# Loading the keys of a multi-head attention in 1 MB transfers with 8192-byte rows, in a kernel that runs two attention blocks on one Trainium2 core

## The chip, the cores and the metric

The kernel runs on one core of one Trainium2 chip. Its time is device microseconds (us) of one execution. In the text, PE is the matrix engine, PEld its weight load, DVE the vector engine, ACT the scalar engine, POOL the GpSimd engine and SP the engine that issues the DMAs. A line number such as L976 is the line of the kernel before; where a line of the changed kernel is meant, the text says so.

## The reference

Two blocks with the same input shapes run side by side and their outputs are put next to each other. Both project x to 32 query heads, attend to a cache of 1024 keys, and project back. Block A shares each of 4 key/value heads among 8 query heads, block B has a key and value head for every query head, so its caches hold 134 MB each (16 x 32 x 1024 x 128 bf16).

```
# A: B, Sq, D = 16, 32, 1024; Hq, Hkv, Sk, Dh = 32, 4, 1024, 128
# B: the same, but with 32 key/value heads
q = (x @ wq).reshape(B, Sq, H, Dh).transpose(0, 2, 1, 3)
scores = einsum("bhqd,bhkd->bhqk", q, k_cache) * Dh ** -0.5
p = softmax(scores, axis=-1)
o = einsum("bhqk,bhkd->bhqd", p, v_cache)
out = o.transpose(0, 2, 1, 3).reshape(B, Sq, H * Dh) @ wo
# result: concatenate([out_A, out_B], axis=-1), bf16
```

## The kernel before

**How the order is made.** The kernel first records all operations in program order, each with its engine, its reads and writes, and the class of buffer it needs (`pr.add`). `list_schedule` then plans them: it takes assumed durations from the table `DUR`, assumed packet times from `PACKET`, and weights from `RANKS` and `TUNE`, and puts out one fixed order for each engine. Operations of engine "any" (copies out of PSUM, the scaling of the output) go to ACT or DVE as the plan sees fit. At run time each engine works through its list in order, and semaphores hold an operation until what it reads has come and what it overwrites has been read. So an instruction that waits holds up all that stands behind it on its engine. SP issues all input DMAs from one queue, in the planned order.

**Block A** works in 128 steps ("quads") of one batch and four heads: keys come in as 256 KB (L891), are transposed on PE (L969), scores are two matmuls of 512 columns (L995), then maximum (L1038), exponential with row sum (L1051), transposes of the probabilities (L1063), the product with the values (L1083), the scaling by 1/sum (L1174 or L1175), and a transpose back (L1182).

**Block B** works in 64 pairs of quads. A pair is two batches of four heads, 2 MB of keys and 2 MB of values. The steps of a pair are these.

- `st_dmaKB` (L910): four DMAs of 512 KB, two heads of one batch each. A partition holds 16 consecutive keys of one head, 4096 bytes, and two heads fill 128 partitions. `KB_sb` has 8 such tiles, so the next pair's keys are under way while one is worked on.
- `st_ktrB` (L976): DVE transposes each tile in place, in 32 x 32 blocks of four-byte elements (two bf16 values each).
- `st_scoresB` (L1027): 64 matmuls on 32 x 32 parts of the PE array, 512 columns each. A quad takes one head parity: its 128 rows are four (batch, head) combinations of 32 queries, its 1024 columns are all keys, in two PSUM banks.
- `st_max` and `st_exp`: one maximum over 1024 columns (L1038) and one exponential over 1024 columns with its row sum (L1051) for each quad.
- `st_ptB` (L1097): eight transposes of the pair's probabilities, and their copies to SBUF (L651, `PT_ev`).
- `st_pvB` (L1116): 64 matmuls of 64 x 64 by 256 columns. The values come in as four DMAs of 512 KB (L955) into `VB_sb`, which has 6 tiles.
- `st_recip` (L1165), `st_norm` (L1174, L1175): one reciprocal and one scaling of 256 columns for each quad.
- `st_otr` (L1190): two matmuls against a selecting matrix `rowsel` for each quad, and a copy into `OTB_sb`, from where `oproj` (L823) projects to the output.

The queries of B are projected by `qprojB` (L754), 128 tokens at a time with the tokens as rows, in `Qtok`. `qprepB_tr` (L765) then transposes them in blocks on DVE, and `qprepB_sh` (L778) moves the blocks between row groups by 16 matmuls with an identity, twice, and two copies into `QR`. This happens once for each group of two pairs, 32 times in all.

The last pair has a function of its own, `st_last` (L1135 and on), which finishes one half of its heads after the other. Near the end of the program tiles for keys and values are also put where weights and queries no longer are needed (`wq_sb`, `xT_sb`, `QT_sb`).

Of the kernel before, what the change touches and what calls it, by code (L numbers as in the profile page):

```python
# [19 lines left out]
NQT = 5  # L20
# [10 lines left out]
PE_MODE = {"scoresB": 2, "Qshuf": 2, "Qshuf2": 2, "PVB": 3, "PVBh": 3}  # L31
MODE_IN = 0.094
MODE_OUT = {0: 0.0, 2: 0.18, 3: 0.1}
PE_INSTR = {"scoresB": 32, "scoresA": 2, "PT_trA": 8, "PT_trB": 8, "PVA": 16, "PVB": 32, "PVBh": 32, "OT_tr": 2, "OT_trB": 4, "KTA_tr": 16, "Qshuf": 16, "Qshuf2": 16,
            "qprojA": 4, "qprojB": 4, "oprojA": 4, "oprojB": 4, "xT_tr": 16}
# [11 lines left out]
TUNE = (6, 7, 1, 5, 6, 8, 8, 8, 8, 8, 8, 11, 5, 15, 1, 9, 0, 1, 5, 1, 7, 14,  # L47
        15, 12, 12, 10, 12, 12, 15, 3, 12, 14, 7, 13, 13, 13, 13, 13, 7, 6, 10, 1, 12, 10,
        3, 12, 0, 11, 9, 12, 7, 13, 12, 11, 12, 3, 4, 10, 14, 9, 9, 10, 4, 0, 0)
# [3 lines left out]
QB0 = [0, 3, 6, 9]  # L53
QA0 = [13 + (i * 12) // 8 for i in range(8)]
QB1 = [27 + (i * 13) // 8 for i in range(8)]
QA_T = [10 + (i * 11) // 8 for i in range(8)]
QB_T = [23 + (i * 15) // 8 for i in range(8)]
# [3 lines left out]
    "scoresB": (0.232, 0.20), "scoresA": (0.216, 0.20), "PT_trA": (0.48, 0.22), "PT_trB": (0.48, 0.22), "PVA": (0.45, 0.22), "PVB": (0.437, 0.22), "PVBh": (0.22, 0.22),  # L61
    "OT_tr": (0.056, 0.22), "OT_trB": (0.112, 0.22), "KTA_tr": (0.45, 0.22), "Qshuf": (0.39, 0.20), "Qshuf2": (0.235, 0.20), "qprojA": (0.432, 0.20), "qprojB": (0.432, 0.20),
    "oprojA": (0.432, 0.20), "oprojB": (0.432, 0.20), "xT_tr": (0.45, 0.22),
    "exp": (1.10, 0.12), "PT_ev@act": (0.466, 0.13), "norm@act": (0.25, 0.13), "normB@act": (0.36, 0.13), "OT_ev@act": (0.11, 0.13), "OTB_ev@act": (0.17, 0.13), "KTA_ev@act": (0.466, 0.13),
    "qA_ev@act": (0.47, 0.13), "qB_ev@act": (0.478, 0.13), "QR_ev@act": (0.478, 0.13), "acc0@act": (0.47, 0.13), "acc0@dve": (0.58, 0.12), "xT_ev@act": (0.90, 0.13),
    "o_fin@act": (0.47, 0.13),
    "KBt_tr": (1.15, 0.11), "max": (1.12, 0.11), "recip": (0.06, 0.11), "norm@dve": (0.265, 0.13), "normB@dve": (0.40, 0.13), "PT_ev@dve": (0.58, 0.12),
    "OT_ev@dve": (0.13, 0.12), "OTB_ev@dve": (0.2, 0.12), "KTA_ev@dve": (0.58, 0.12), "QBt_tr": (0.345, 0.10), "acc+": (0.58, 0.12), "accF": (0.59, 0.12),
    "qA_ev@dve": (0.58, 0.12), "qB_ev@dve": (0.58, 0.12), "xT_ev@dve": (0.60, 0.12), "o_fin@dve": (0.58, 0.12), "QR_ev@dve": (0.58, 0.12),
# [3 lines left out]
PACKET = {"kb_dma": (4096, 0.1592), "vb_dma": (4096, 0.1592), "outh_dma": (1024, 0.049), "wqh_dma": (1024, 0.049)}  # L73
# [41 lines left out]
SLOTS = {"bank": 8, "P": 2, "P2": 1, "PT": 2, "PT2": 2, "stat": 8, "O": 2, "O2": 3}  # L115
# [12 lines left out]
class Prog:  # L128
# [63 lines left out]
    def _needs_wait(self, op, d):  # L192
        if d.dma_key is not None:
            return True
        if d.eng != op.eng:
            return True
        if (d.name, op.name) == ("Qshuf", "Qshuf2"):
            return True
        return op.eng in self.SELF_SYNC
# [49 lines left out]
    def list_schedule(self, lat=0.05, look=LOOK):  # L249
# [170 lines left out]
        while True:  # L420
# [61 lines left out]
            for u in users[best]:  # L482
                uo = ops[u]
                same_pe = (op.dma_key is None and beng == uo.eng and uo.eng == "pe" and uo.name != "Qshuf2")
# [68 lines left out]
def build(nc, pa, pb, out):  # L553
# [34 lines left out]
    with stack:  # L588
# [12 lines left out]
        Qtok = sb("Qtok", [P, NQT, CW], BF)  # L601
        QBt = sb("QBt", [P, CW], BF)
        QR = sb("QR", [P, 2, 4, 2, Dh], BF)
# [11 lines left out]
        P2_sb = sb("P2_sb", [P, SLOTS["P2"], 2 * Sk], BF)  # L615
        PT2_sb = sb("PT2_sb", [P, SLOTS["PT2"], Sk], BF)
        O2_sb = sb("O2_sb", [P, SLOTS["O2"], 2, Dh], BF)
        rowsel = sb("rowsel", [P, 2, P], BF)
        PT_sb = sb("PT_sb", [P, SLOTS["PT"], NCH, P], BF)
        O_sb = sb("O_sb", [P, SLOTS["O"], Dh], BF)  # L620

# [121 lines left out]

        def qprojB(m_, G):
            c2, mh = m_ // 2, m_ % 2
            lazy_flush(("wq", 1, c2))

            JS = 2 if DJ % 2 == 0 else 1
            v = Virt("bank", "pj")
# [653 lines left out]
```

## Time and profile before

| | |
|---|---|
| Time, median of 2 runs | 850.95 us (847.71 to 854.19) |
| Profiled execution, its own time | 851.34 us |
| Span in its profile | 849.5 us |
| Busy: PE, DVE, ACT, POOL | 783.0, 727.0, 623.6, 6.1 us |
| Mean granted PE clock | 0.995 |
| Moved by DMA | 341.68 MB, 402 GB/s over the span |

The span is what the profiler saw from the first instruction to the last; the execution's own time is 1.8 us longer. Busy time counts an instruction from its start to its end, so neighbours on one engine may overlap, and a busy PE need not be at its peak. A row of the groups names line, engine, operation, output and input, shape and count; behind the bar stand the busy time, the mean duration in ns, and the idle time just before them with what ended it.

### The profile page before, as it was taken

How to read it: one execution, taken by the hardware profiler on the slowest of the kernel's cores; microseconds unless marked ns; L12 is line 12 of the kernel's file. 1: busy time of each engine (PE TensorE's matmuls, PEld its weight loads, DVE VectorE, ACT ScalarE, POOL GpSimd, SP SyncE). 2: the span in 40 equal slices, each digit the busy share in tenths (PEclk: the TensorE clock that was granted, in tenths of full speed). 3: DMA queues.
4: the chain of work that ended last, by engine and by line, in shares of the span. 5: the costliest groups of instructions: out<-in, count | busy, mean ns of one | idle time of the engine just before them, and what ended most of it. 6: DMA issues, size and time to landing. Idle time of an engine off the chain costs nothing.

```text
span 849.5 us, 29749 instructions
## 1 busy us (share of the span) xinstructions
PE 783.0 (92%) x13056; PEld 522.6 (62%) x13056; DVE 727.0 (86%) x1018; ACT 623.6 (73%) x1363; POOL 6.1 (1%) x20
## 2 busy tenths in 40 slices
PE   7989999999898999998999988999899998899878
PEld 4456665666565566665666665666666666666655
DVE  1499987979799898987999898998999978998995
ACT  3497787778677777786788787677877867686874
POOL 1000000000000000000000000000000000000000
PEclk9999999999999999999999999999999999999999
DMA  9999999999999999999999999999999999999995
GB/s 339 415 412 414 411 411 410 405 393 394 416 384 412 409 395 415 416 398 412 414 392 408 411 392 416 415 416 405 410 402 415 412 414 415 415 400 414 416 418 226
DMA packets 112208, 341.68 MB, mean 402 GB/s; under 512 B 12048, under 2 KB 12304, under 8 KB 112080
## 3 DMA queue, kind: packets, MB, share of 16 engines
q1 hardware_dynamic: 111520, 337.95, 100.0%
q8 instruction: 103, 1.69, 0.7%
q0 software_dynamic: 560, 1.84, 0.5%
q14 instruction: 25, 0.20, 0.1%
HBM read 337.64 MB, written 2.10 MB: 400 GB/s over the span
## 4 chain that ended last, share of the span: by engine, by line
PE 55%; DVE 23%; ACT 14%; DMA 5%; issue 2%; SPq 1%; DVEq 0%; ACTq 0%
DVE stat L1038 10%; PE psum L1116 10%; PE psum L823 10%; DVE KB_sb L976 8%; ACT P_sb L1051 8%; PE psum L1027 6%; PE psum L1063 5%; PE psum L754 5%; PE psum L1097 5%; PE psum L1083 4%; DMA KB_sb<-in_B_k_cache_dram 4%; PE psum L995 4%; PE psum L735 4%; ACT PT_sb L651 2%; ACT O_sb L1174 1%
## 5 line engine op out<-in xcount | busy, mean ns | idle before, releaser
L1038 DVE TENSOR_REDUCE stat<-psum 128x1 f32<-128x1024 f32 x256 | 303.6, 1210 | 50.7 <-PE psum L995 31.5
L1051 ACT ACTIVATE P_sb<-psum,stat 128x1024 bf16<-128x1024 f32 x246 | 275.9, 1122 | 63.2 <-DVE stat L1038 59.7
L976 DVE STREAM_TRANSPOSE KB_sb<-KB_sb 128x1024 f32<-128x1024 f32 x240 | 286.6, 1222 | 6.2 <-DMA KB_sb<-in_B_k_cache_dram 6.0
L651 ACT COPY PT_sb<-psum 128x512 f32<-128x512 f32 x226 | 131.4, 604 | 35.2 <-PE psum L1063 22.0
L1116 PE MATMUL psum<-VB_sb,PT_sb 64*64 64x256 bf16 x3584 | 116.2, 271 | 8.6 <-ACT P_sb L1051 5.2
L1116 PEld LDWEIGHTS psum<-VB_sb,PT_sb 64*64 64x64 bf16 x3584 | 97.0, 107 | 27.7 <-issue 25.5
L1174 ACT ACTIVATE O_sb<-psum,stat 128x128 bf16<-128x128 f32 (+1 forms) x205 | 80.8, 417 | 43.2 <-PE psum L1083 23.1
L1063 PE MATMUL psum<-id,P_sb 128*128 128x128 f32 x512 | 88.7, 297 | 6.9 <-ACT P_sb L1051 4.1
L1063 PEld LDWEIGHTS psum<-id,P_sb 128*128 128x128 f32 x512 | 74.0, 208 | 25.2 <-ACT P_sb L1051 13.8
L995 PE MATMUL psum<-KTA_sb,QT_sb 128*128 128x512 bf16 x256 | 84.4, 384 | 3.1 <-ACT P_sb L1051 1.6
L1083 PE MATMUL psum<-VA_sb,PT_sb 128*128 128x128 bf16 x1024 | 78.8, 221 | 7.5 <-ACT P_sb L1051 2.6
L1083 PEld LDWEIGHTS psum<-VA_sb,PT_sb 128*128 128x128 bf16 x1024 | 63.2, 99 | 31.6 <-issue 12.0
L1027 PE MATMUL psum<-KB_sb,QR 32*32 32x512 bf16 x3840 | 73.3, 394 | 8.1 <-ACT P_sb L1051 4.6
L1097 PE MATMUL psum<-id,P_sb 128*128 128x128 f32 x472 | 76.2, 287 | 4.1 <-ACT P_sb L1051 3.5
L754 PE MATMUL psum<-wq_sb,xT_sb 128*128 128x512 bf16 x256 | 72.4, 394 | 3.3 <-DMA wq_sb<-in_B_wq_dram 1.6
L1097 PEld LDWEIGHTS psum<-id,P_sb 128*128 128x128 f32 x472 | 63.8, 193 | 17.3 <-ACT P_sb L1051 7.5
L823 PE MATMUL psum<-woB_sb,OTB_sb 128*128 128x512 bf16 x256 | 66.9, 380 | 2.4 <-ACT P_sb L1051 1.7
L1027 PEld LDWEIGHTS psum<-KB_sb,QR 32*32 32x32 bf16 x3840 | 43.8, 89 | 35.3 <-ACT P_sb L1051 8.3
L823 PE MATMUL psum<-woA_sb,OTA_sb 128*128 128x512 bf16 x256 | 62.8, 380 | 0.4 <-ACT OTA_sb L651 0.3
L735 PE MATMUL psum<-xT_sb,wq_sb 128*128 128x512 bf16 x192 | 54.2, 380 | 1.7 <-issue 1.2
L1051 ACT ACTIVATION_READ_ACCUMULATOR P_sb<-psum,stat 128x1 f32 x246 | 50.3, 205 | 0.0
L835 DVE TENSOR_TENSOR acc<-acc,psum 128x512 f32<-128x512 f32 x64 | 41.3, 675 | 9.6 <-PE psum L823 9.4
(74 smaller groups left out, 720.2 us busy)
## 6 DMA issues: line engine op xcount, KB each, us to landing
KB_sb<-in_B_k_cache_dram SPq DMA_DIRECT2D x240, 512.0 KB, 8.9
VB_sb<-in_B_v_cache_dram SPq DMA_DIRECT2D x234, 512.0 KB, 7.8
KA_sb<-in_A_k_cache_dram SPq DMA_DIRECT2D x64, 256.0 KB, 7.8
VA_sb<-in_A_v_cache_dram SPq DMA_DIRECT2D x64, 256.0 KB, 8.0
wq_sb<-in_B_wq_dram SPq DMA_DIRECT2D x16, 512.0 KB, 8.3
woB_sb<-in_B_wo_dram SPq DMA_DIRECT2D x32, 256.0 KB, 8.5
woA_sb<-in_A_wo_dram SPq DMA_DIRECT2D x32, 256.0 KB, 7.0
wq_sb<-in_B_k_cache_dram SPq DMA_DIRECT2D x16, 512.0 KB, 11.5
```

Source lines behind the costliest of these rows:

```text
L651: return e.copy(dst, src) if hasattr(e, "activation") else e.tensor_copy(dst, src)
L754: last = e.matmul(bank(v)[:, 0:CW], xT_sb[:, 1, j, G * P:(G + 1) * P], wq_sb[:, j, mh * CW:(mh + 1) * CW], start=(j == 0), stop=(j == DJ - 1))
L823: last = e.matmul(bank(v)[:, 0:OUTW], OT[:, gp, hh, :], wo_[:, hh, oh * OUTW:(oh + 1) * OUTW], start=(hh == 0), stop=(hh == nh - 1))
L976: pr.add("dve", lambda e: e.transpose(tile_k(x).bitcast(F32), tile_k(x).bitcast(F32)), writes=[home_k(x)], name="KBt_tr", rtag={home_k(x): ...
L995: pr.add("pe", lambda e, u=u: e.matmul(bank(vS[u]), qt[:, q.b, q.hh0:q.hh0 + 4, :].rearrange("p a q -> p (a q)"), KTA_sb[:, sl, u * 512:(u ...
L1027: last = e.matmul(bank(q.vS[g2])[32 * x:32 * x + 32, :].rearrange("p (s j) -> p s j", s=16), lhsT, rhs, start=(fp == 0), stop=(fp == 3), t ...
L1038: pr.add("dve", lambda e: e.tensor_reduce(stat[:, vst.idx, 0:1], both(vS), AXIS.XY, ALU.max, negate=True), writes=vS + [vst], name="max")
L1051: return e.activation(dst, src, ACTF.Exp, bias=stat[:, vst.idx, 0:1], scale=1.0, accum_out=stat[:, vst.idx, 1:2])
L1063: last = e.transpose(bank(vb)[:, m * P:(m + 1) * P], p32[:, m:Sk // 2:NPK], id32[:])
L1083: last = e.matmul(bank(vb)[:, 0:Dh], ptc_of(vPT, c, 0, P), VA_sb[:, kvs, c, :], start=(c == 0), stop=(c == NCH - 1))
L1097: last = e.transpose(bank(vb)[:, m * P:(m + 1) * P], p32[:, 4 * h + m:Sk:8], id32[:])
L1116: last = e.matmul(bank(q.vbo)[n0:n0 + 64, 0:2 * Dh].rearrange("p (i d) -> p i d", i=2), pt2_chunk(vPT, c, e0, n0), v2[e0:e0 + 64, :, c, :] ...
```

## The change

Keys of B now come in as one DMA for a batch and four heads: 1 MB, 128 rows of 8192 bytes. A head lies in 32 partitions (one row group of the PE array), and a partition holds 32 consecutive keys. The in-place transpose takes the four-byte elements in another order, so that the bf16 values of one block stand four apart instead of two. The rows of the scores change their meaning: a quad is now two heads of the pair's two batches, and the keys of a head are split into two halves (`u`) that lie in different rows, of which each has its own maximum for each of the two score banks.

What follows from that: the maximum over two banks gives two columns; the exponential is two instructions of 512 columns, each with its own bias and sum; the two halves of a head's keys are brought together by weights exp(m - m'), worked out on POOL with copies between groups of 32 partitions, one small exponential on ACT and one reciprocal on DVE (`st_weights`); the product with the values leaves twice as much output (the two key halves in separate rows, for two heads), so there are four scalings of 256 columns for each pair instead of two; and the selecting matmuls, now eight of 64 columns for each pair, also add the two halves.

The queries of B are projected with the weights as the stationary operand, every fourth column of them, so that the result already has the rows that the scores need (`QR`). The block transposes on DVE, the matmuls with the identity and their copies fall away. Values come in as before in 512 KB, but two tiles belong to one quad, and the products of a quad wait for its own two tiles alone. `st_last` goes, the last pair runs through the same functions quad by quad. The tables of the plan are set anew.

The core of the diff, without the tables of the plan:

```diff
-        def qprojB(m_, G):
+        def qprojB(m_, f, t0=0, tn=NTOK):
...
-                        last = e.matmul(bank(v)[:, 0:CW], xT_sb[:, 1, j, G * P:(G + 1) * P], wq_sb[:, j, mh * CW:(mh + 1) * CW], start=(j == 0), stop=(j == DJ - 1))
+                        last = e.matmul(bank(v)[:, 0:tn], wq_sb[:, j, mh * CW + f:(mh + 1) * CW:4], xT_sb[:, 1, j, t0:t0 + tn], start=(j == 0), stop=(j == DJ - 1))
...
+            evac(QR[:, m_ % 2, f, t0:t0 + tn], lambda: bank(v)[:, 0:tn], reads=[], writes=[v] + res, name="qB_ev" if tn > P else "qB0_ev",
-        def qprepB_tr(m_, G):
-        def qprepB_sh(m_, G):
...
+        def st_dmaKB(y):
+                src = pb["k"][q.b0 + y % 2, q.m * MS:(q.m + 1) * MS].rearrange("h (p s) d -> (h p) (s d)", s=32)
...
         def st_ktrB(x):
-            pr.add("dve", lambda e: e.transpose(tile_k(x).bitcast(F32), tile_k(x).bitcast(F32)),
+            pairs = lambda: tile_k(x).bitcast(F32).rearrange("p (s j g) -> p s g j", s=16, g=2)
+            pr.add("dve", lambda e: e.transpose(pairs(), pairs()),
...
# st_scoresB
-                            rhs = tile_k(4 * q.pn + x)[r0:r0 + 32, :].rearrange("p (s x) -> p s x", s=16)[:, :, o0:o0 + 63:2]
+                                rhs = kt_.rearrange("p (s v x) -> p s v x", s=16, v=2)[:, :, u, fp::4]
...
# st_max, block B
+                pr.add("dve", lambda e: e.tensor_reduce(stat2[:, q.vB.idx, 2 * q.e:2 * q.e + 2], both(vS), AXIS.X, ALU.max, negate=True),
# st_exp, block B
+            def emitB(e):
+                for g2 in range(2):
+                    k_ = 2 * q.e + g2
+                    src = bank(vS[g2]).rearrange("p (a s j) -> p j a s", a=2, s=8)
+                    dst = p2_of(vP)[:, g2 * 512:(g2 + 1) * 512].rearrange("p (j a s) -> p j a s", a=2, s=8)
+                    last = e.activation(dst, src, ACTF.Exp, bias=stat2[:, q.vB.idx, k_:k_ + 1], scale=1.0, accum_out=stat2[:, q.vB.idx, 4 + k_:5 + k_])
+                return last
+        def st_weights(qs, early):
+            vB = qs[0].vB
+            S = lambda a: stat2[:, vB.idx, 4 * a:4 * a + 4]
+            V = [q.vst for q in qs]
+            def swap(lo):
+                for b in range(4):
+                    pr.add("pool", lambda e, b=b: e.tensor_copy(stat2[32 * (b ^ 1):32 * (b ^ 1) + 32, vB.idx, lo + 8:lo + 12], stat2[32 * b:32 * b + 32, vB.idx, lo:lo + 4]),
+                           reads=V if lo else [q.vmx for q in qs], writes=[vB, "pool"], name="swap")
+            if early:
+                swap(0)
+                pr.add("pool", lambda e: e.tensor_tensor(S(4), S(0), S(2), ALU.subtract), writes=[vB, "pool"], name="small")
+                pr.add("pool", lambda e: e.tensor_scalar(S(4), S(4), 80.0, None, ALU.min), writes=[vB, "pool"], name="small")
+                pr.add("act", lambda e: e.activation(S(4), S(4), ACTF.Exp), writes=[vB], name="expw")
+                return
+            swap(4)
+            pr.add("pool", lambda e: e.tensor_tensor(S(4), S(4), S(3), ALU.mult), writes=[vB, "pool"], name="small")
+            pr.add("pool", lambda e: e.tensor_tensor(S(4), S(4), S(1), ALU.add), reads=V, writes=[vB, "pool"], name="small")
+            pr.add("dve", lambda e: e.reciprocal(S(5), S(4)), writes=[vB], name="recip")
...
# st_pvB, for one quad
-            for c0 in range(0, 16, 4):
+            for c0 in range(0, 8, 4):
+                            last = e.matmul(bank(vbo[h_])[n0:n0 + 64, i * 2 * Dh:(i + 1) * 2 * Dh], pt2_chunk(vPT, c, e0, n0),
+                                            v2[e0:e0 + 64, c * 2 * Dh:(c + 1) * 2 * Dh], start=(c == 0), stop=(c == 7), tile_position=(e0, n0))
+        def st_normB(q, vbo, h_, eng="any"):
+                    return e.activation(dst, src, ACTF.Copy, scale=stat2[:, vB.idx, 20 + k_:21 + k_])
+        def st_otrB(qs, vbo, h_, eng=None):
+                        last = e.matmul(bank(vbo[h_])[:, x * 64:x * 64 + 64], O2_sb[:, q.vO[h_].idx, u, :], rowsel[:, u, :], start=(u == 0), stop=(u == 1))
...
# pairB
+            for q in qs:
+                st_max(q)
+            st_weights(qs, True)
             for q in qs:
-                st_max(q)
                 st_exp(q)
-            st_ptB(qs)
+            st_weights(qs, False)
+            for q in qs:
+                st_ptB(q)
...
-            for q in qs:
-                st_recip(q)
-                st_norm(q)
-                st_otr(q)
+            for h_ in range(2):
+                for q in qs:
+                    st_normB(q, vbo, h_)
+                st_otrB(qs, vbo, h_)
```

## The prediction

> **What bounds the kernel now.** First the top of the page, to see which resource is full.
>
> ```profile
> span 849.5 us, 29749 instructions
> ...
> PE 783.0 (92%) x13056; PEld 522.6 (62%) x13056; DVE 727.0 (86%) x1018; ACT 623.6 (73%) x1363; POOL 6.1 (1%) x20
> ...
> DMA  9999999999999999999999999999999999999995
> GB/s 339 415 412 414 411 411 410 405 393 394 416 384 412 409 395 415 416 398 412 414 392 408 411 392 416 415 416 405 410 402 415 412 414 415 415 400 414 416 418 226
> ...
> q1 hardware_dynamic: 111520, 337.95, 100.0%
> ...
> PE 55%; DVE 23%; ACT 14%; DMA 5%; issue 2%; SPq 1%; DVEq 0%; ACTq 0%
> ```
>
> All 16 DMA engines are busy in every slice but the last. The trace's packet records say it more sharply: between 20 and 830 us the engines' time without a packet sums to only 2.3 us of all sixteen; after 830 us it is 8.5 us. So the transfers set the pace, at about 415 GB/s where packets are 4096 B, and the span is these bytes plus some 11 us of gaps, mostly the end.
>
> The chain of work in the last line names DMA for only 5%. The waits of the issuing queue explain that.
>
> ```profile
> SPq L955 <- PE psum L1116: 109.9, 36, 6.9
> SPq L891 <- PE psum L969: 80.9, 34, 6.7
> SPq L910 <- PE psum L1027: 57.0, 24, 5.1
> SPq L898 <- PE psum L1083: 54.2, 15, 8.3
> ```
>
> SP waits for PE to give a buffer back (us in total, times, longest), and the chain goes through PE there. Issues of 512 KB land after 7.8 to 8.9 us by the page, while the bytes need 1.25 us; the rest is mostly queue, which covers the waits. On the other side, by the landing events, a value tile's first matmul starts 14.5 us after its landing at the median, a key tile's transpose 2.4 us, and one in ten under 0.2 us. Keys are thus the link where transfers and compute touch. Compute has little room: PE is busy 47 of 50 us in the middle stretches. A gain in transfers is one only if PE, DVE and ACT keep up.
>
> **The change part by part.** The durations:
>
> ```profile
> L976 DVE STREAM_TRANSPOSE KB_sb<-KB_sb 128x1024 f32<-128x1024 f32 x240 | 286.6, 1222 | 6.2 <-DMA KB_sb<-in_B_k_cache_dram 6.0
> L1051 ACT ACTIVATE P_sb<-psum,stat 128x1024 bf16<-128x1024 f32 x246 | 275.9, 1122 | 63.2 <-DVE stat L1038 59.7
> ...
> L1051 ACT ACTIVATION_READ_ACCUMULATOR P_sb<-psum,stat 128x1 f32 x246 | 50.3, 205 | 0.0
> ...
> L1174 ACT ACTIVATE O_sb<-psum,stat 128x256 bf16<-128x256 f32 x82 | 36.5, 475 | 17.2 <-PE psum L1116 14.3 <-PE psum L995 1.4 <-DVE stat L1165 1.2
> ...
> L651 ACT CAST QR<-psum 128x512 bf16<-128x512 f32 x56 | 31.2, 599 | 7.3 <-PE psum L778 7.2
> ...
> L778 PE MATMUL psum<-QBt,ident 32*32 32x256 bf16 x512 | 20.1, 279 | 3.3 <-issue 0.4 <-ACT P_sb L1051 0.3
> ...
> L765 DVE STREAM_TRANSPOSE QBt<-Qtok 128x256 f32<-128x256 f32 x32 | 13.6, 425 | 13.6 <-ACT Qtok L649 13.6
> ...
> L640 POOL COPY rowsel<-ident 32x32 bf16<-32x32 bf16 x4 | 0.8, 202 | 0.2
> ```
>
> And the weight loads of L671, from the answer on that line (lowest/median/highest ns):
>
> ```profile
> L671 PEld LDWEIGHTS psum<-ident,acc x64: 142/147/171, 3.6 to 17.8; 128*128 128x128 bf16 x64
> ```
>
> *Key transfers, on the path.* Before, 256 DMAs of 128 packets of 4096 B, 2048 per DMA engine; after, 128 DMAs, 1024 packets of 8192 B per engine. Packet records give medians of 159 ns for 4096 B, 84 ns for 2048 B and, for the 25 packets of 8192 B that fetch instructions in mid-run, 309 ns. 2048 x 159 = 325.6 us becomes 1024 x 309 = 316.4: -9.2. Each DMA also ends in a 4-byte record of 9 ns per engine: 128 fewer, -1.2. Sum -10.4. The upper bound is 0: the DMA share in 50-us stretches reads 1.02 to 1.03, so packets overlap and a part of the fixed cost may already be hidden. I take -10, nearer the direct row, since all records of an engine sum to 853.9 us against 838 us not idle, a factor of only 0.98.
>
> *Later first key tile.* Both halves of 1 MB land together, so the first of two transposes may start 1.25 us later. The tiles' release does not change: one pair's scores read all four, before and after. A shift of the loop costs once, but one in ten starts is without slack: between 0 and 64 x 0.2 x 1.25 = 16 us. I take +2, about once more the present 2.3 us of gaps.
>
> *ACT, beside the path.* By the built order: 256 exponentials of 512 columns for 128 of 1024. A 512-column copy is 0.60 us, so each is 0.60 + 0.21, and 256 x 0.81 - 128 x 1.33 = +37. Scalings of 256 columns go from 82 to 211 on ACT: +61. The 64 small exponentials are not in the trace: at least a 64-column copy's 0.2, so +13, at most a 512-column copy's 0.6 (+38); 0.2 is nearer. Query copies on ACT fall from 84 to 28 (six of them short): -34. The plan moves other copies to DVE: -22. Sum +55: 679 us, 81% of 840.
>
> *DVE, beside the path.* -14 (L765), 64 fewer reciprocals -9, fewer query copies -3, moved copies about +25: 726 us, 86% of 840. Maxima keep 1024 elements and their 1.21 us. The key transposes read and write at 8-byte steps, which no row of DVE shows. The nearest is PE's weight load with 16-byte steps (L671): 147 ns at the median against 98 with contiguous data (L969), 50% more. Bounds: 0 and 256 x 0.61 = +156. I take 0, the step being half of L671's.
>
> The Trainium skill (Advanced Engine Details and Errata, SBUF Cachelines) states that two hits on each 16-byte line keep full speed, and fewer do not. Steps of 8 bytes give two, so by the rule these transposes cost 0 more; 16 bytes give one, and L671 agrees with that. No run here shows 8 bytes on DVE.
>
> *PE.* -20 (L778), with its switching of tile sizes. Selecting matmuls go from 252 to 512, half as wide: today 0.11 us of busy time each, so between 0 and +29. Projection issues 32 more short matmuls, +3. Between -17 and +12, and I take -5: 778 us, 93% of 840. Scores read at 8-byte steps, before at 4. Their 64 matmuls take 1.2 us a pair, so one of the 16 array parts has 0.3 us for a stream of 0.21 us (128 to 512 columns adds 0.16 us between L969 and L995): bounds 0 and, with doubled streams, +0.5 a pair, 32 us. I take 0. Weight loads of the projection at 8-byte steps (98 to 147 ns) hide behind 380-ns matmuls.
>
> *POOL, a new chain.* Twelve small operations a pair, each waiting for the one before: 202 ns (L640) to 311 ns (its slowest row), plus 0.1 to 0.2 between. The six after the second exponential end 2 us later, then the reciprocal on DVE; in that time PE transposes (0.7), a copy follows (0.6) and the products run (1.0), 2.3 us in all. So the chain hides behind these, barely; without the cover a scaling waits at the head of ACT's list, with the next maxima's exponentials behind it. The early chain ends in a small exponential on ACT in the same way.
>
> *SP* issues 128 fewer; *values* are freed per quad, earlier: both 0. The start stays full of transfers. From the last landing (840.8 us) to the end the order of work is much the same: 0, within 1 us.
>
> *Sum.* With less room on ACT I add +2 for further gaps: -10 + 2 + 2 = -6. The profiled execution took 851.3, so 845.3, and it lay 0.4 us above the median of the runs: 845 us.
>
> **The rivals.**
>
> *Compute takes the gain back.* For: the chain is 92% compute, and PE stays at 93%. If ACT's +55 shows by its 14% of the chain (+8) and PE's +12 by its 55% (+7), then -10 + 15 = +5: 856 us. Against: DVE waits for keys without slack, so a part does reach compute. The case that 8192-B data packets cost as much as two of 4096 belongs here: -1 + 4, 854 us.
>
> *Strided reading, slower.* The key transposes at 8-byte steps. It decides where DVE's 726 us pass 95% of 850, i.e. from +82 us, 0.32 us (26%) each. With the 50% of L671 DVE needs 882 us, and at 95% full the kernel takes 928. For: no row excludes it. Against: half the step of L671. Doubled score streams alone would give PE 810 us, some 870.
>
> *The POOL chain, slower.* If its operations take 0.5 us, the chain needs 4 us instead of 2, and the scalings of each pair hold ACT and two PSUM banks 0.5 to 2 us. ACT has 160 us free, so from about 1 us a pair it shows: at half of 64 x 0.75, 845 + 24 = 869 us. For: POOL is idle today, so its cost beside a busy DVE is unseen. Against: 202-ns rows.
>
> The Trainium skill (GPSIMD Engine Reference, Specifications) has POOL and DVE contend where DVE reads two SBUF inputs or runs in a two-port mode. DVE here reads one SBUF input at a time, so by it this chain stays short; no run here shows it yet.
>
> *A gain over 2%.* It would need 17 us, more than the transfers give; only a shorter end (8 us from the last landing) could add to it.
>
> **How the numbers follow.** Forecast 0.48 (its own range 839 to 851), gain taken back 0.26 (850 to 862), POOL 0.13 (855 to 885), strided reading 0.09 (865 to 930), over 2% 0.04. The range 837 to 870 leaves out most of strided reading, a third of POOL and a little at the bottom. Two per cent, 17 us, is about what a measurement of this kernel can tell from no change. Faster by more: 0.04. Slower by more (over 868): 0.08 of strided reading and 0.06 of POOL, 0.14. Within: 0.82.
>
> **What would show it.** Right: the GB/s row rises to 420 or more in slices full of keys, key packets at 309 ns, DMA still 9 in all slices; transposes at 1.22 us and scores at 0.39; POOL operations near 0.2 us; ACT near 680 us busy. Wrong: DMA digits below 9 in mid-run, SP or ACT waits that name POOL, L976's successor well above 1.22 us, or ACT's scalings with much idle time before them.

## The result and the profile after

The changed kernel takes 912.27 us (911.88 to 912.66, two runs) beside 850.95: a ratio of 1.072, 95% interval 1.068 to 1.076. It is 61 us slower; forecast were 845 us and a range of 837 to 870.

The top of the page of the changed kernel (the 40 slices are now 22.8 us each):

```profile
span 910.9 us, 30094 instructions
...
PE 840.0 (92%) x12768; PEld 531.5 (58%) x12768; DVE 734.3 (81%) x974; ACT 659.5 (72%) x1697; POOL 150.8 (17%) x788
...
DMA  9999999999999999899999999799999999999982
GB/s 341 419 416 411 389 377 339 386 415 356 359 383 419 372 371 401 327 396 389 368 361 410 380 405 400 271 384 396 397 346 418 412 389 408 396 375 403 384 338 99
...
q1 hardware_dynamic: 93088, 337.94, 95.2%
...
PE 63%; ACT 21%; DVE 9%; DMA 5%; issue 2%; SPq 1%; DVEq 0%; ACTq 0%
```

PE's busy time has grown by 57 us (783.0 to 840.0), the span by 61. The transfers no longer set the pace. The DMA row hardly shows it, with its digit still 9 in all but the last two slices and two in mid-run; the GB/s row does, with 271 to 390 in about half of its slices, where before all but the first and the last read 384 to 418. Queue q1 has gone from 100.0% to 95.2%. PE has gone from 55% of the chain to 63%, and ACT from 14% to 21%.

The groups with their shapes kept apart say which work grew. First the score matmuls of the kernel before, then the kernel after. There, L1009 are the score matmuls (L1027 before), L953 the key transposes, L1040 and L1033 the exponentials of B and A, L1142 the scalings of B, L1056 the POOL copies and L1067 the reciprocal behind them:

```profile
L1027 PE MATMUL psum<-KB_sb,QR 32*32 32x512 bf16 x3840 | 73.3, 394 | 8.1 <-ACT P_sb L1051 4.6 <-issue 0.9 <-ACT PT_sb L651 0.9
```

```profile
L953 DVE STREAM_TRANSPOSE KB_sb<-KB_sb 128x1024 f32<-128x1024 f32 x240 | 287.8, 1225 | 10.8 <-DMA KB_sb<-in_B_k_cache_dram 10.7
L1040 ACT ACTIVATE P_sb<-psum,stat 128x512 bf16<-128x512 f32 x236 | 160.0, 693 | 20.2 <-DVE stat L1024 19.3
L1009 PE MATMUL psum<-KB_sb,QR 32*32 32x512 bf16 x3840 | 124.2, 622 | 7.1 <-ACT P_sb L1033 3.7 <-issue 1.6 <-ACT OTB_sb L650 1.0
L1056 POOL COPY stat<-stat 32x4 f32<-32x4 f32 x512 | 92.0, 180 | 724.0 <-DVE stat L1024 525.8 <-ACT stat L1062 147.0 <-DVE stat L1163 27.9
L1142 ACT ACTIVATE O_sb<-psum,stat 128x256 bf16<-128x256 f32 x211 | 88.3, 480 | 18.2 <-PE psum L1128 15.4 <-DVE stat L1067 1.4 <-DVE stat L1163 0.8
L1067 DVE RECIPROCAL stat<-stat 128x4 f32<-128x4 f32 x64 | 10.3, 161 | 8.3 <-POOL stat L1066 8.1
```

The score matmuls are the row that stands out: 622 ns for 394, and 124.2 us busy for 73.3, with the same count and shape. The key transposes use the same 8-byte step and take 1225 ns for 1222. Two lines of each kernel's timeline (start in us, duration in us, a set of 64 score matmuls) show the same from outside, before first, then after:

```profile
197.40 1.22 PE L1027 MATMUL psum<-KB_sb,QR 32*32 32x512 bf16 x64
209.67 1.22 PE L1027 MATMUL psum<-KB_sb,QR 32*32 32x512 bf16 x64
```

```profile
197.34 2.02 PE L1009 MATMUL psum<-KB_sb,QR 32*32 32x512 bf16 x64
216.95 2.03 PE L1009 MATMUL psum<-KB_sb,QR 32*32 32x512 bf16 x64
```

A set is four rounds over the 16 array parts. In the trace nine in ten rounds start 222 to 251 ns apart before, 431 to 455 ns after. A set takes 0.82 us more at the median, and 64 sets give 52 us.

The waits, first one of before, then those of after: who waited for whom, the total in us, how often, the longest. DVE's maxima of B now wait 74.1 us for the scores, where they waited 16.0:

```profile
DVE stat L1038 <- PE psum L1027: 16.0, 25, 2.1
```

```profile
DVE stat L1024 <- PE psum L1009: 74.1, 58, 3.3
...
SPq L931 <- PE psum L1128: 204.6, 77, 7.3
...
SPq L883 <- PE psum L1009: 69.7, 28, 6.3
```

SP too waits longer for PE to give value tiles (L931, L1128 are the products) and key tiles (L883) back: 204.6 us for 109.9, and 69.7 for 57.0. Before, the GB/s row stayed up through such waits; now it dips.

### The profile page after: what moved, and what is told of

Read it like the earlier page. It is cut to its first block, busy times and chain, and to the rows that moved or that the text cites. A ratio compares the mean times of both kernels' runs of the same rounds, so it can differ in the third digit from the quotient of the medians.

```text
span 910.9 us, 30094 instructions
## 1 busy us (share of the span) xinstructions
PE 840.0 (92%) x12768; PEld 531.5 (58%) x12768; DVE 734.3 (81%) x974; ACT 659.5 (72%) x1697; POOL 150.8 (17%) x788
## 3 DMA queue, kind: packets, MB, share of 16 engines
q1 hardware_dynamic: 93088, 337.94, 95.2%
## 4 chain that ended last, share of the span: by engine, by line
PE 63%; ACT 21%; DVE 9%; DMA 5%; issue 2%; SPq 1%; DVEq 0%; ACTq 0%
PE psum L1009 14%; PE psum L1128 12%; ACT P_sb L1040 10%; PE psum L796 10%; PE psum L1111 6%; PE psum L1078 5%; DVE stat L1024 4%; PE psum L1098 4%; DMA KB_sb<-in_B_k_cache_dram 4%; PE psum L972 4%; PE psum L734 3%; PE psum L754 3%; ACT P_sb L1033 3%; DVE KB_sb L953 2%; ACT O_sb L1142 2%; PE psum L945 2%
## 5 line engine op out<-in xcount | busy, mean ns | idle before, releaser
L953 DVE STREAM_TRANSPOSE KB_sb<-KB_sb 128x1024 f32<-128x1024 f32 x240 | 287.8, 1225 | 10.8 <-DMA KB_sb<-in_B_k_cache_dram 10.7
L1056 POOL COPY stat<-stat 32x4 f32<-32x4 f32 x512 | 92.0, 180 | 724.0 <-DVE stat L1024 525.8
L1024 DVE TENSOR_REDUCE stat<-psum 128x2 f32<-128x1024 f32 x128 | 150.9, 1218 | 74.3 <-PE psum L1009 74.1
L1040 ACT ACTIVATE P_sb<-psum,stat 128x512 bf16<-128x512 f32 x236 | 160.0, 693 | 20.2 <-DVE stat L1024 19.3
L1021 DVE TENSOR_REDUCE stat<-psum 128x1 f32<-128x1024 f32 x128 | 154.2, 1208 | 12.9 <-PE psum L972 12.2
L1033 ACT ACTIVATE P_sb<-psum,stat 128x1024 bf16<-128x1024 f32 x128 | 144.4, 1128 | 23.8 <-DVE stat L1021 22.4
L1009 PE MATMUL psum<-KB_sb,QR 32*32 32x512 bf16 x3840 | 124.2, 622 | 7.1 <-ACT P_sb L1033 3.7
L1128 PE MATMUL psum<-VB_sb,PT_sb 64*64 64x256 bf16 x3584 | 116.8, 272 | 0.2
L1128 PEld LDWEIGHTS psum<-VB_sb,PT_sb 64*64 64x64 bf16 x3584 | 91.0, 107 | 23.8 <-issue 15.8
L1142 ACT ACTIVATE O_sb<-psum,stat 128x256 bf16<-128x256 f32 x211 | 88.3, 480 | 18.2 <-PE psum L1128 15.4
L1111 PE MATMUL psum<-id,P_sb 128*128 128x128 f32 x472 | 82.5, 299 | 13.9 <-ACT P_sb L1040 11.2
L1078 PE MATMUL psum<-id,P_sb 128*128 128x128 f32 x512 | 89.1, 298 | 4.4 <-ACT OTB_sb L650 1.4
L1078 PEld LDWEIGHTS psum<-id,P_sb 128*128 128x128 f32 x512 | 73.3, 208 | 26.9 <-issue 9.2
L1009 PEld LDWEIGHTS psum<-KB_sb,QR 32*32 32x32 bf16 x3840 | 48.4, 88 | 52.8 <-issue 23.2
L754 PE MATMUL psum<-xT_sb,wq_sb 128*128 128x512 bf16 (+2 forms) x288 | 71.6, 365 | 3.6 <-DMA wq_sb<-in_B_wq_dram 2.8
L1171 ACT ACTIVATE O_sb<-psum,stat 128x128 bf16<-128x128 f32 x111 | 42.1, 380 | 35.0 <-PE psum L1098 31.5
```

What stands on the lines that cost most here:

```text
L953: pr.add("dve", lambda e: e.transpose(pairs(), pairs()), writes=[home_k(x)], name="KBt_tr", rtag={home_k(x): x}, wtag={home_k(x): ("T", x)})
L1009: last = e.matmul(bank(q.vS[g2])[n0:n0 + 32, :].rearrange("p (s j) -> p s j", s=16), QR[r0:r0 + 32, gp, fp, tok:tok + 32], rhs, start=(fp ...
L1021: pr.add("dve", lambda e: e.tensor_reduce(stat[:, vst.idx, 0:1], both(vS), AXIS.XY, ALU.max, negate=True), writes=vS + [vst], name="max")
L1024: pr.add("dve", lambda e: e.tensor_reduce(stat2[:, q.vB.idx, 2 * q.e:2 * q.e + 2], both(vS), AXIS.X, ALU.max, negate=True), writes=vS + [q ...
L1033: return e.activation(dst, src, ACTF.Exp, bias=stat[:, vst.idx, 0:1], scale=1.0, accum_out=stat[:, vst.idx, 1:2])
L1040: last = e.activation(dst, src, ACTF.Exp, bias=stat2[:, q.vB.idx, k_:k_ + 1], scale=1.0, accum_out=stat2[:, q.vB.idx, 4 + k_:5 + k_])
```

## The experiments

Each kernel was timed against the kernel before on the same chip; ratios carry their 95% intervals, and differences in us are between medians. The kernel before lay between 849.54 and 851.78 us on these chips, so that much of a difference between two experiments can be the chip's.

| kernel | us | ratio |
|---|---|---|
| e1: changed, scores two values apart | 872.95 | 1.027 (1.022 to 1.031) |
| e2: before, four apart | 890.09 | 1.048 (1.044 to 1.051) |
| e3: e1, keys in 4096-byte packets | 873.34 | 1.028 (1.025 to 1.032) |
| e5: changed, plan knows the score time | 953.98 | 1.123 (1.117 to 1.129) |
| e6: e1, one exponential a quad | 862.24 | 1.015 (1.013 to 1.017) |
| e7: e1, no weights on POOL | 873.07 | 1.028 (1.024 to 1.032) |
| e8: e1, order searched anew | 877.29 | 1.030 (1.026 to 1.033) |
| e9: before, exponentials in halves | 874.73 | 1.028 (1.024 to 1.033) |
| e11: changed, plan knows, order searched anew | 891.42 | 1.046 (1.042 to 1.049) |
| e12: e6, scalings of 16 columns | 859.89 | 1.009 (1.006 to 1.013) |
| e13: before, keys land by two | 887.23 | 1.043 (1.040 to 1.045) |
| e14: e6, 1 MB as two landings | 863.74 | 1.015 (1.013 to 1.018) |
| e15: before, order searched anew | 857.03 | 1.007 (1.004 to 1.009) |
| e16: before, order unsearched | 883.64 | 1.039 (1.036 to 1.041) |
| e17: e1, order unsearched | 932.14 | 1.097 (1.093 to 1.101) |

### The step of the scores' operand: e1 and e2

e1 lets the transpose write each block's two halves one behind the other. The matmuls then read every second value, as before the change.

```diff
-            pr.add("dve", lambda e: e.transpose(pairs(), pairs()),
+            halves = lambda: tile_k(x).bitcast(F32).rearrange("p (s g j) -> p s g j", s=16, g=2)
+            pr.add("dve", lambda e: e.transpose(halves(), pairs()),
...
-                                rhs = kt_.rearrange("p (s v x) -> p s v x", s=16, v=2)[:, :, u, fp::4]
+                                o0 = (fp // 2) * 64 + fp % 2
+                                rhs = kt_.rearrange("p (s v x) -> p s v x", s=16, v=2)[:, :, u, o0:o0 + 63:2]
```

> The changed kernel with one thing undone: the block transpose of the keys writes its two halves next to each other, so that the score matmuls read bf16 values 4 bytes apart again instead of 8. Order, loads and all other work are those of the changed kernel. Theory 'stream' (the 32x32 score matmuls pass their 512 columns at half speed at 8-byte steps, 0.82 us more for each of 64 pairs, and PE has no room for it): score matmuls back at 0.39 us, PE busy near 790 us, time near 912 - 52 = 860 us, between 845 and 868. Rival 'load' (the doubled scalings, the halved exponentials and the POOL chain hold the kernel up): the time stays above 890 us though the matmuls are short again.

e2 gives the kernel before the four-apart step and leaves all else. The step is in the transposes of keys and queries and in both operands of the score matmuls; the lines here show the moving one.

```diff
-                            rhs = tile_k(4 * q.pn + x)[r0:r0 + 32, :].rearrange("p (s x) -> p s x", s=16)[:, :, o0:o0 + 63:2]
+                            rhs = tile_k(4 * q.pn + x)[r0:r0 + 32, :].rearrange("p (s x) -> p s x", s=16)[:, :, o0:o0 + 125:4]
```

> The kernel before with the same step alone: block transposes of keys and queries in the changed kernel's order of elements, and score matmuls that read both operands 8 bytes apart. 512 KB loads, one maximum, no POOL work. Theory 'stream': score matmuls 0.62 us, PE busy near 835 us, time 851 + 52 = 903 us, between 890 and 915. Rival 'load': within 1% of 851 us, since nothing but the step has changed.

From the two pages, first PE's busy line and the score group of e1, then those of e2:

```profile
PE 792.7 (91%) x12768; PEld 527.9 (61%) x12768; DVE 731.8 (84%) x974; ACT 658.8 (76%) x1697; POOL 150.8 (17%) x788
...
L1011 PE MATMUL psum<-KB_sb,QR 32*32 32x512 bf16 x3840 | 74.9, 393 | 9.6 <-ACT P_sb L1035 4.5 <-issue 3.3 <-ACT OTB_sb L650 1.0
```

```profile
PE 830.8 (94%) x13056; PEld 530.0 (60%) x13056; DVE 728.6 (82%) x1018; ACT 623.6 (70%) x1363; POOL 6.1 (1%) x20
...
L1029 PE MATMUL psum<-KB_sb,QR 32*32 32x512 bf16 x3840 | 123.5, 626 | 8.3 <-ACT P_sb L1053 4.3 <-ACT PT_sb L651 1.6 <-issue 1.2
```

The step alone takes the matmul from 394 to 626 ns in one kernel, and its removal takes it from 622 to 393 ns in the other. That it is the moving operand's step is shown by e1, which leaves the other operand as it is. In e2 the weight loads grow too, from 89 to 103 ns, but a set takes 2.04 us at the median, where the changed kernel with its contiguous weights takes 2.03.

The step is worth 39 us of the changed kernel (912.27 to 872.95) and 40 us of the kernel before (850.39 in those runs to 890.09), each in the order that it came with. This is the larger part of the 61. It is less than the 52 us that theory 'stream' took, so e1 lies above its range (845 to 868), and well under the rival's 890.

### Is it the order instead? e5 and e11

The plan still believed 0.232 us for one of its items, which is 16 score matmuls (e11's expectation says 32). e5 tells it 0.44 and leaves TUNE.

```diff
-    "scoresB": (0.232, 0.20), ...
+    "scoresB": (0.44, 0.20), ...
```

> The changed kernel with one entry of the plan's duration table set to what the score matmuls take in its profile (0.44 us for 16 of them instead of 0.232); the work is the same, only the order differs. Theory 'stream' (raw PE time): the time stays within 12 us of 912. Rival 'plan' (the order, made with too short a duration, wastes PE): at least 25 us of the 61 come back.

953.98 us: 42 us worse with a truer duration, which neither theory had foreseen. The likely reason is that TUNE was searched for one set of durations, and another duration moves the later choices; e11 bears it out. So e5 says nothing on the step, but shows how much an order can cost. e11 repeats it with TUNE searched anew, tells the plan 1.33 us for the two exponentials as well, and sets the plan's latency `lat` to 0.085 us instead of 0.05, as e8 below does:

```diff
-    "scoresB": (0.232, 0.20), ... "expB": (1.20, 0.12), ...
+    "scoresB": (0.45, 0.20), ... "expB": (1.33, 0.12), ...
-TUNE = (15, 14, 8, 15, ...
+TUNE = (11, 14, 8, 3, ...
```

> The changed kernel as it is, scores at 8-byte steps, with a new order: the plan is told 0.45 us for 32 score matmuls (it had 0.232) and 1.33 us for the two exponentials, and TUNE was searched anew for these. Theory that the 8-byte step is work that PE cannot hide (52 us more of busy time on an engine at 92%): it stays 20 us or more above e8, at 875 to 890 us. Rival, the loss is a matter of the order, which was made for the shorter scores: it comes down to e8's time within 8 us. Rival as in e5 (new order, 954 us): above 912 us.

891.42 us. A new order wins back 21 us, but e11 stays 14 us above e8, which has the same treatment and the short step, and 18 above e1. This lies between its theory (20 us or more above e8) and its rival (within 8). Where both orders are searched anew, then, the step costs 14 us and not 39: it does not vanish, but more than half of its cost hangs on the order.

### The packets: e3

e1 with the 1 MB transfers landing in two tiles that are not neighbours, so that each row is cut into two packets of 4096 B. The eight loads of keys that land in `wq_sb` near the end stay whole.

```diff
-                dst = ... dst[:, sl:sl + 2, :].rearrange("p i x -> p (i x)")
+                dst = ... dst.rearrange("p (v s) x -> p s v x", v=2)[:, sl // 2, :, :]
```

> As e1, but each 1 MB load of keys goes into two tiles that are not neighbours, so that it is made of 4096-byte packets; the order of all engines is the same. If transfers bound e1, the shorter packets cost the 9 us of the prediction's term and the time is e1 + 9 (between +5 and +11). If compute bounds e1, the time is e1 within 3 us and the DMA engines of e1 have gaps that are filled here.

The GB/s rows of e1 and of e3:

```profile
GB/s 341 418 414 418 408 419 378 387 415 399 373 397 415 387 401 380 361 404 365 409 380 411 382 387 420 381 310 415 416 414 419 414 418 419 415 412 416 419 410 159
```

```profile
GB/s 337 416 413 415 414 416 392 375 412 400 373 388 414 405 406 391 357 406 373 374 373 413 399 401 416 366 321 414 413 415 416 413 415 417 417 416 415 417 417 148
```

The times are equal within their scatter. In the eleven full slices from the 28th to the 38th the mean is 416.1 GB/s with 8192-byte packets and 415.3 with 4096: 0.2%, or 2 us of a run.

### The POOL chain: e7

e1 without the POOL operations and without the small exponential; the weights that bring the two key halves together are left out.

```diff
+            if name in ("swap", "small", "expw"):
+                continue
```

> e1 without the weights between the key halves: the copies and small operations on POOL and the small exponential on ACT fall away, and the reciprocal is taken of the plain sums; the order of all else is kept. It leaves out bringing the two halves to one maximum. Rival 'chain': at least 8 us come back, 855 to 866. Theory 'ACT': 64 small exponentials of 0.14 us and a few waits go, 2 to 6 us, 867 to 871.

873.07 us beside e1's 872.95: neither 'chain' nor 'ACT' had that. The chain of 768 POOL instructions, 144 us busy, is worth nothing, and neither are the 64 small exponentials.

### The halved exponentials: e6 and e9

e6 is e1 with one exponential of 1024 columns for each quad of B, in the same order; the second half's own maximum and sum are left out.

```diff
-                for g2 in range(2):
-                    k_ = 2 * q.e + g2
-                    src = bank(vS[g2]).rearrange("p (a s j) -> p j a s", a=2, s=8)
...
+                k_ = 2 * q.e
+                src = both(vS).rearrange("p g (s j) -> p g j s", s=16)
```

> e1 with one exponential of 1024 columns for a quad of block B, with the first half's maximum and one sum, instead of two of 512; the same order on every engine. It leaves out the second half's own maximum and sum. In e1 two half exponentials hold ACT for 1.33 us a quad (start to next start), one whole one for 1.10, and the plan reckons 1.20. Theory 'ACT' (that the halves, 0.23 us longer for each of 128 quads, are a main part of the 22 us by which e1 stays above the kernel before): at least 8 us come back, 855 to 866 us. Rival 'chain' (POOL's weights and the waits on them): within 4 us of 873.

e9 does the reverse in the kernel before: two of 512, with the same bias; the second sum is left out of the scaling.

```diff
-                    src = both(vS).rearrange("p g (s j) -> p g j s", s=16)
+                    for g2 in range(2):
+                        src = bank(vS[g2]).rearrange("p (s j) -> p j s", s=16)
```

> The kernel before with the exponential of block B as two instructions of 512 columns, with the same maximum for both; the order is kept. It leaves out adding the second sum. Theory 'ACT': the 0.23 us for each of 128 quads shows here as well, in part, since ACT had room: 856 to 866 us. If ACT's room hides it, within 3 us of 851.

The exponential groups of e9:

```profile
L1052 ACT ACTIVATE P_sb<-psum,stat 128x512 bf16<-128x512 f32 x236 | 160.9, 691 | 36.0 <-DVE stat L1038 33.0
L1054 ACT ACTIVATE P_sb<-psum,stat 128x1024 bf16<-128x1024 f32 x128 | 144.3, 1129 | 24.2 <-DVE stat L1038 23.6
```

e6 wins 11 us of e1, as theory 'ACT' had it. e9 loses 25 us (849.54 in those runs to 874.73), more than either of its theories allowed. From start to start in the trace, two halves take 1.33 us and a whole takes 1.10: 0.23 us, 29 us over 128 quads. ACT is busy for only 75% of e9's span, yet nearly all of the 29 us reach its end.

### The doubled scalings: e12

e6 with only 16 of the 256 columns of each scaling of B; the other 240 stay unscaled, at zero.

```diff
-                dst = O2_sb[:, vO.idx, :, :].rearrange("p u d -> p (u d)")
-                src = bank(vbo[h_])[:, i * 2 * Dh:(i + 1) * 2 * Dh]
+                dst = O2_sb[:, vO.idx, 0, 0:16]
+                src = bank(vbo[h_])[:, i * 2 * Dh:i * 2 * Dh + 16]
```

> e6 (862.24 us: scores two values apart, one exponential of 1024 columns a quad) with its 256 scalings of block B cut from 256 columns to 16; the other 240 columns are not scaled (they stay zero). The order is that of e6. In e6 the scalings of B take 109 us of ACT and DVE (211 and 45 of them), in the kernel before 57 us (82 and 44); at 16 columns I estimate 0.25 us each, 64 us, from the 128-column row's 0.375 and the 256-column row's 0.48. Theory that the doubled scalings are the 12 us that e6 still lies above the kernel before: 848 to 853 us. Rival, the order of the work and its gaps are the rest: 858 to 863 us. In between: both.

This brings the scalings of B from 109 us of ACT and DVE to 56, as much as in the kernel before (57). The ratio falls from 1.0151 to 1.0091, about 5 us, with intervals that just part: between the theory and its rival. So the scalings are some of the 12 us left in e6, and some 8 us remain.

The profile of e12 says where a part of them lies. It is of its fastest run, 855.04 us, with a span of 853.3. By the landing events its last load lands at 840.9 us, as in the kernel before (840.8). So nearly all of the 3.8 us that its span is longer come behind the last landing: 12.3 us to the end instead of 8.7.

### The landing of 1 MB: e13 and e14

e13 is the kernel before, in its order, with the first transpose of each two also waiting for the second tile.

```diff
+            more = tuple((kind, sl + 1) for kind, sl in writes if sl % 2 == 0) if name == "KBt_tr" else ()
-            newp.add(eng, emit, actual(reads), actual(writes), dma_key, name, dur, tag, prio)
+            newp.add(eng, emit, actual(reads) + more, actual(writes), dma_key, name, dur, tag, prio)
```

> The kernel before, in its own order, in which the transpose of the first key tile of each two also waits for the landing of the second, as a 1 MB transfer makes it wait. Nothing else changes. The prediction's term 'later first key tile' was +2 us with bounds 0 and 16. Theory that it is a main part of what e6 and e12 still lie above the kernel before (DVE's waits on key landings rose from 6 to 22 us there): +6 to +15 us, 857 to 866 us, with DVE's wait on the key landings near 20 us. Rival, keys land early enough: 0 to +3 us, 850 to 854 us.

e14 is e6 with each 1 MB issued as two DMAs of 4096-byte rows, one for each tile.

```diff
+            if name == "kb_dma":
+                for h_ in range(2):
+                    kind, sl = writes[h_]
+                    newp.add(eng, lambda e, h_=h_, emit=emit: emit(e, h_), (), (writes[h_],), f"{kind.lower()}{sl}", name, dur // 2, tag, prio)
+                continue
```

> e6 (862.24 us, ratio 1.0151 to the kernel before: scores two values apart, one exponential a quad, the second half's own maximum and sum left out) with each 1 MB key load issued as two of 512 KB, one for each tile, in the same place of SP's order; all other engines keep their order. Theory that the common landing costs: 850 to 857 us, ratio 1.000 to 1.007, DVE's wait on key landings back from 22 to under 12 us. Rival, the 64 landings come early enough and the waits on keys come from full queues: 860 to 865 us, ratio 1.012 to 1.018, or a little more for 128 more issues on SP.

DVE's waits for key landings, in the kernel before and in e13, then in e6 and in e14:

```profile
DVE KB_sb L976 <- DMA KB_sb<-in_B_k_cache_dram: 6.0, 6, 3.1
DVE KB_sb L977 <- DMA KB_sb<-in_B_k_cache_dram: 43.7, 21, 4.9
```

```profile
DVE KB_sb L954 <- DMA KB_sb<-in_B_k_cache_dram: 21.6, 16, 4.8
DVE KB_sb L962 <- DMA KB_sb<-in_B_k_cache_dram: 15.7, 11, 3.6
```

In the kernel before the wait costs 36 us (6.0 us of waits became 43.7), more than either of e13's theories had. In e6 its removal brings nothing (ratio 1.0152 beside 1.0151), though the waits fall from 21.6 to 15.7 us. The order of the changed kernel was planned with common landings, that of the kernel before was not. As a cause of the 61 us the landing is ruled out as far as e6 goes.

### Form or order: e8, e15, e16, e17

e8 is e1 with the plan told 1.33 us for the two exponentials, and TUNE searched anew; e15 is the kernel before with TUNE searched anew in the same way; both also set `lat` to 0.085 instead of 0.05. e16 and e17 set every entry of TUNE to 0, in the kernel before and in e1.

```diff
# e8, from e1
-TUNE = (15, 14, 8, 15, ...
+TUNE = (1, 14, 13, 12, ...
# e16, from before; e17, from e1
+TUNE = (0,) * 80
```

> The changed kernel with the scores' operand two values apart (e1, 872.95 us), and its fixed order worked out anew: the plan is told the measured 1.33 us for the two exponentials of a quad of B (it had 1.20), and its table TUNE was searched anew for that. The same instructions, another order. Theory that the rest of the loss is an order that no longer fits (issue gaps, waits of ACT in places where the plan had none): 853 to 862 us, the loss against the kernel before within 1%, PE's idle time in mid-run down. Rival, the added work of ACT and DVE itself bounds (ACT 659 us, DVE 730 us, each waiting for the other in a cycle over two score banks): no order helps, 868 to 878 us. Second rival, as in e5: any new order is worse than one that was searched on the chip: over 885 us. I give them 0.5, 0.25, 0.25.

> The kernel before with another order: its table TUNE was searched anew in the same way as for e8, the same instructions otherwise. If the order that the kernel before has is one of many good ones, 847 to 856 us; if a new order costs the kernel before as much as it cost e1 in e8 (+4) or more, 855 to 885 us, and then the 8 to 12 us that e6 and e12 still lie above the kernel before are within what an order is worth.

> The kernel before with every entry of TUNE at 0: the plan's first choice of weights throughout, no search. Theory that the order is worth a few per cent: 875 to 930 us. Rival, under 865 us: the order matters little.

> e1 (changed kernel, scores two values apart, 872.95 us) with every entry of TUNE at 0, to be held against e16. Theory that the changed kernel's form itself costs some 2% whatever the order: 15 us or more above e16. Rival, that the remaining loss is the better searched order of the kernel before: within 8 us of e16 or below it.

A new order didn't help e1 (877.29 us): the theory that was given 0.5 missed. The same search cost the kernel before 6 us. With the same search the forms lie 20 us apart (877.29 and 857.03), with no search 48 us (932.14 and 883.64), and with the orders that they came with 22. So with the step repaired the changed form is slower under every order tried: the loss isn't just a well-searched order of the kernel before. But a second searched order lay 4 us above the first in e1 and 6 us in the kernel before, and the 8 us left after e12 are not far from that.

**The account.** 61 us, in the orders that the two kernels came with: 39 for the step of the score operand (e1, with e2 in agreement), 10 to 11 for the halved exponentials (e6), about 5 for the doubled scalings (e12), nothing for POOL (e7), packets (e3) or the common landing (e14). Some 8 us stay open. In e12's profiled run what remains lies in the end; the other runs, 4.8 us above it at the median, have no trace, and the order is a rival that is not ruled out. No version that beats the kernel before was found.

## Why the prediction was wrong

*What bounds the kernel: right, and drawn from too little.* The DMA engines were full, and the prediction said that a gain counts only if PE, DVE and ACT keep up. It turned this round only inside a rival ("some 870"). PE was busy for 92% of the span, and of the 52 us more of score work the transfers did not hide 39 (e1).

*The failed step: "Scores read at 8-byte steps, before at 4 ... bounds 0 and, with doubled streams, +0.5 a pair, 32 us. I take 0."* The streams nearly doubled, and a pair's set took 0.82 us more, 52 us in all. The choice of 0 had no row behind it, while the only strided PE row at hand, L671, showed a loss. The upper bound was too low as well: it gave an array part 0.3 us of room, the set's 1.2 us divided by four, but the set lasts until the last matmul, 0.39 us long, has ended. The rounds themselves start 222 to 251 ns apart before, about the stream's 0.21 us. So there was hardly any room, and four rounds of 0.2 us more give the 0.82. The likelier mechanism in "strided reading" was taken to be DVE's; it was PE's, whose price there ("some 870") was 20 us too low for the step alone (e2: 890). The rest of PE's work, taken as -5 between -17 and +12, stayed inside its bounds: with the short step PE is busy 792.7 us (e1), 10 more than before.

*Key transposes, +0: right.* 1225 ns for 1222. The rule quoted from the Trainium skill (Advanced Engine Details and Errata, SBUF Cachelines), that two hits on a 16-byte line keep full speed, held for DVE. It didn't hold for PE's moving operand, with the same two hits: there the measurement decides (622 ns for 394). The prediction weighed the rule for DVE alone and let the score operand go without it.

*Projection weights at 8-byte steps, "98 to 147 ns", hidden: right.* The answers on the line, before and after (lowest, median, highest ns):

```profile
L754 PEld LDWEIGHTS psum<-wq_sb,xT_sb x256: 95/98/151, 7.1 to 697.8; 128*128 128x128 bf16 x128
```

```profile
L754 PEld LDWEIGHTS psum<-xT_sb,wq_sb x288: 110/113/153, 6.4 to 750.5; 128*128 128x128 bf16 x144
```

113 ns, beside matmuls of 381 (512 columns).

*Transfers, -10: the packet was right, its worth wrong.* Key packets took 309 ns at the median, but the rate of full slices rose by 0.2% (e3), not 1.2%. The other end of the term's range, 0, was the right one. The prediction's reason for that end, that packets of one engine overlap and hide a part of their fixed cost, fits; no run tests it.

*Later first key tile, +2 (0 to 16): right for this kernel by e14, outside its bounds for the old order (e13, +36).* The bounds come from 12.8 starts late by 1.25 us each. In e13 DVE waited 21 times and 2.1 us in the mean, 4.9 at the longest.

*ACT, +55 "beside the path": its size was high, its place wrong.* It came to 659.5 us, +36. But 10 to 11 us (e6) and about 5 (e12) of it reached the end, and the halves in the kernel before 25 (e9). An engine with a quarter of its time free isn't off the path when it stands between score banks that PE needs and maxima that DVE makes. The rival "compute takes the gain back" had this mechanism, with +8 for ACT.

*DVE 726 and POOL hidden: right.* DVE came to 734.3 us; POOL copies took 180 ns and its other operations 198 to 219; the reciprocal waited 8.1 us for POOL in all, and e7 puts the chain at nothing. No contention with DVE showed: its maxima of B took 1218 ns beside the busy POOL, all maxima before 1210. The rule (the Trainium skill, GPSIMD Engine Reference, Specifications) has POOL contend with DVE instructions that read two SBUF inputs or run in a two-port mode. The trace agrees for a DVE that reads one, as long as none of its instructions here runs in such a mode.

*The end, "0, within 1 us": wrong.* By the landing events the kernel before ends 8.7 us after its last landing and the changed kernel 17.7 us after (893.1 to 910.9 us), so 9 of the 61 us lie there. With the short step it is 13.1 us (e1). The order alone can make as much: the kernel before with no search (e16) needs 17.6 us from its last landing to its end. The last pair also lost its own function `st_last`; no run tells the two apart.

## What to carry to other kernels

An operand's step is a property of the engine that reads it: price it for each engine from a row with that step, and where there is no row, let the doubled stream be the bound and compare it with the interval between instructions, not with the set's mean. A full DMA queue does not hide work on an engine that is 92% busy: 52 us more on PE cost 39 and 40 us in orders made without them, and still 14 where both orders were searched anew. A fixed order belongs to the durations that it was searched for, so compare two forms with the same effort spent on both orders.

## What was not expected of the hardware

- bf16 matmuls on 32 x 32 parts stream at about half rate when the moving operand's values lie 8 bytes apart: 431 to 455 ns from round to round for 512 columns, 222 to 251 at 4 bytes.
- Longer rows brought next to nothing: a full queue moved 415.3 GB/s in 4096-byte packets and 416.1 in 8192-byte ones.
- Two exponentials of 512 columns with sums take 1.33 us where one of 1024 takes 1.10.
- The DMA row stays at 9 while the rate falls, since packet records grow longer where it does: in the changed kernel the mean of 4096-byte packets is 159 ns in the second slice, at 419 GB/s, and 191 in the seventh, at 339, and both slices show a 9.
- A slow stretch can follow a short stall of PE. Stretches of e1: start, end and length, busy us and instructions of PE, PEld, DVE, ACT and POOL, then the granted clock, the DMA share and GB/s:

```profile
370.00:380.00 10.00, 8.89 (x121) 6.39 (x119) 8.50 (x10) 9.12 (x25) 2.25 (x12) 1.00 1.03 419
380.00:383.00 3.00, 1.23 (x69) 0.73 (x62) 1.28 (x2) 1.57 (x4) 0.00 (x0) 1.00 1.01 394
383.00:390.00 7.00, 6.04 (x32) 3.49 (x32) 3.51 (x3) 2.71 (x8) 1.14 (x6) 0.51 1.01 411
390.00:400.00 10.00, 9.57 (x155) 6.17 (x157) 7.82 (x13) 7.89 (x19) 1.14 (x7) 1.00 0.93 332
```

After 1.23 us of work in 3 us the clock is 0.51 for 7 us, in which PE does 32 matmuls. Apart from the end of the span, the kernel before and the changed one have two stretches at half clock each and e1 three, this one 6.8 us long and the others 3.4. In the 3 us ahead of each PE was busy for 0.8 to 2.0. They cost some us a run, and are no part of the main difference.
